# Second chunk's transposes on the DMA queue, logits in groups of two products, and the last residual added at evacuation

## The chip, the cores and the metric

The kernel runs on one core of one Trainium2 chip. The metric is the device time of one execution in microseconds (us), median of several runs. Engines are called by the names of the profile: PE is TensorE (PEld its weight loads), DVE is VectorE, ACT is ScalarE, POOL is GpSimd, SP is SyncE, which here only issues DMAs. A "q" after the name (SPq, ACTq) means the engine's instruction queue when it issues a DMA.

## The reference

The input is 2048 tokens of width 640 in bfloat16. Each row is normalised to xn, and the result is the sum of three parts: x itself, an attention branch and a feed-forward branch, both on xn.

```python
qkv = xn @ wqkv                       # 32 heads of 20
idx = pos[:, None] - 2*arange(8)      # each token sees itself and 7 others, 2 apart
logits = einsum(q, k[idx]) * 20**-0.5 # -1e9 where idx < 0
o = einsum(softmax(logits), v[idx])
h = gelu(xn @ w1 + b1)                # 640 -> 1536
out = x + o @ wo + (h @ w2 + b2)
```

## The kernel before

**Chunks and blocks.** The 2048 tokens are four chunks of 512 (n = 0 to 3), each of four blocks of 128 (bl = 0 to 3). Activations are held transposed, features on partitions and tokens along the free axis, so that a chunk's projection is a matmul with 512 columns.

**Stages of one chunk.** Statistics of x (st, DVE) and their square root (ACT) give xn (chunk 0 on DVE, the others on ACT, L398 to L409). xn has two buffers. It is then transposed into xnT: for chunks 0 and 1 by five PE matmuls a block against an identity (tp, L416) and an ACT copy from PSUM (tc, L420), for chunks 2 and 3 by a DMA transpose that SP issues (td, L428). Fifteen projections give q, k and v (for chunk 0 per block: gj, L472; for others pj, L455), copied out by ACT (pc, L490).

**Attention.** For each of the eight offsets w, DVE multiplies q with a shifted k (qk, L505). Two offsets share one product tile; there are four such tiles (pool "prod"), which also serve the products with v. A logits task (lg, L517) sums the 20 features of each head of one product tile by 20 matmuls with a 128x32 matrix of ones: 5 feature tiles times 4 token blocks, each block written to its own 32 partitions of L. In chunk 0 a mask is added to L for the first tokens by one more matmul for each two product tiles (L527). Then follow maximum (m, L540), difference (z, L547), exponential (ACT), sum, reciprocal and the weights attn on DVE. DMAs on SP and ACT repeat attn over the features of a head (ax, L584), DVE multiplies with shifted v (av, L600), adds (L609), and writes oT (L615), which has one buffer.

**Feed-forward and output.** Twelve tasks f1 (L622) with a GELU each (ge, ACT, L633) give hT; 18 buffers hold hT. A block's output needs five tasks o (pc 0 to 4; L655 for columns 0 to 511, "lo", L657 for the other 128, "hi"): pc 0 to 3 multiply hT with w2, pc 4 multiplies oT with wo. ACT copies lo and hi to osb (oc, L662), and a DMA issued by POOL adds osb to the output in memory (od, L668). What it adds to was stored before: x + b2, computed on DVE from x_sb and b2bc (xb, L432) and stored by SP (L439). The very last block, LASTB, does not go this way: its x + b2 is not stored, but added in PSUM, by two matmuls of x_sb against the identity, in pc 3:

```python
if pc == 3 and n * BPC + bl == LASTB:
    srcs.append((ident[:], x_sb[:, n * BPC + bl, :]))
```

Its lo half is computed first, copied by ACT and stored by SP (oclo, L676), while its hi half is still computed (ohi); then DVE copies hi (ochi, L685) and ACT's queue stores it.

**Order.** All instructions of PE, DVE and ACT are issued in one fixed order per engine, found when the kernel is built. `make_plan` adds tasks with an engine, an assumed duration, a rank, the tasks they need, the buffers they hold, and for some a time `after` which they may start. `Plan.run` then plays time forward: whenever an engine is free it starts the ready task with the smallest rank for which buffers are left. The table RANK adds offsets to the ranks of named groups ("f12" is all f1 of chunk 2). On the chip only the order remains: each instruction starts when what it needs is there, and everything behind it on its engine waits with it. A fourth kind of task, "dq", stands for the DMA queue in the plan.

**Loads.** Before anything else SP issues all loads in this order: x of chunk 0 and wq, wk, wv, then b1, x of the other chunks, w1, w2, wo and b2bc (L316 to L329). SP is not among the engines with a fixed order; 40 matmuls on the identity (L694) open PE's work.

Of the kernel before, what the change touches and what calls it, by code (L numbers as in the profile page):

```python
# [11 lines left out]
ALU = mybir.AluOpType  # L12
# [6 lines left out]
class Plan:  # L19
# [37 lines left out]
    def run(self):  # L57
        end, left, held = {}, list(self.tasks), {p: {} for p in self.pools}
        remaining = {b: set(u) for b, u in self.bufs.items()}
        free = {PE: 0.0, VE: 0.0, SE: 0.0, DQ: 0.0}  # L60
        now, started, table = 0.0, [], "sqrt"
        running, slacks = [], {t["slack"] for t in self.tasks}
        while left:
            done = [t for t in running if t["end"] <= now + 1e-9]
            for t in done:
                running.remove(t)
                for b in t["bufs"]:
                    remaining[b].discard(t["name"])
                    if not remaining[b]:
                        held[b[0]].pop(b, None)  # L70
            moved = True
            while moved:
                moved = False
                for eng in (PE, VE, SE, DQ):
                    if free[eng] > now + 1e-9:
                        continue
                    best = None
                    for t in left:
                        if t["eng"] != eng or t["after"] > now:
                            continue  # L80
                        if best is not None and (t["rank"], t["i"]) >= (best["rank"], best["i"]):
                            continue
                        if any(
                            n not in end
                            or end[n] + t["slack"] + (self.LAG[self.by[n]["eng"]] if self.by[n]["eng"] != eng else 0.0) > now + 1e-9
                            for n in t["needs"]
                        ):
                            continue
                        new = {}
                        for b in t["bufs"]:  # L90
                            if b not in held[b[0]]:
                                new[b[0]] = new.get(b[0], 0) + 1
                        if any(len(held[p]) + k > self.pools[p] for p, k in new.items()):
                            continue
                        best = t
                    if best is not None:
                        left.remove(best)
                        best["start"], best["end"] = now, now + best["us"]
                        if best["table"] not in (None, table):
                            table = best["table"]  # L100
                            best["end"] += self.TABLE
                        end[best["name"]] = best["end"]
                        free[eng] = best["end"]
                        for b in best["bufs"]:
                            held[b[0]][b] = True
                        running.append(best)
                        started.append(best)
                        moved = True
            nxt = [f for f in free.values() if f > now + 1e-9]
            for late in slacks:  # L110
                ready = [e + late + self.LAG[self.by[n]["eng"]] for n, e in end.items()]
                nxt += [r for r in ready if r > now + 1e-9]
            nxt += [t["after"] for t in left if t["after"] > now + 1e-9]
            if left and not nxt:
                raise RuntimeError("no piece can start: " + ", ".join(t["name"] for t in left[:8]))
            if left:
                now = min(nxt)
        return started
# [3 lines left out]
P = 128  # L122
# [16 lines left out]


RANK = {
    "ad00": 178, "av2": 376.9, "f11": 47.4, "f12": 101.9, "f13": 56.6, "gj1": 41.2, "gj3": 41.9, "o01": -41.2,
    "o02": 33.3, "o13": 84.5, "o23": 46.4, "ot0": 75.1, "pc12": 58.9, "pj30": 33.5, "pj32": 57, "qk2": -89.4,
    "st2": 250.4, "tc1": -2.9, "xb0": 48.2,
}


def make_plan(fns, offsets=RANK):
# [16 lines left out]
    for n in range(NCH):  # L165
# [15 lines left out]
        for bl in range(BPC):  # L181
            xn, tp = ("xn", n, bl), ("acc", "tp", n, bl)
            pl.add(f"xn{n}{bl}", SE if n else VE, 0.81 if n else 0.42, early + -4.0 if n else -99, [f"rc{n}" if n else f"rc{n}{bl}"], f("xn", n, bl), [xn])
            if n > 1:
                pl.add(f"tc{n}{bl}", DQ, 4.0, early - 3.0, [f"xn{n}{bl}"], f("td", n, bl), [xn, xnT])
                continue
            pl.add(f"tp{n}{bl}", PE, 0.3, early + -3.0 if n else -99, [f"xn{n}{bl}"], f("tp", n, bl), [xn, tp])
            pl.add(f"tc{n}{bl}", SE, 0.65, early + -3.0 if n else -99, [f"tp{n}{bl}"], f("tc", n, bl), [tp, xnT])
        pl.add(f"xb{n}", VE, 1.43, base + 36, [f"xn{n}{bl}" for bl in range(BPC)], f("xb", n), after=32.0)

        if n == 0:
            for bl in range(BPC):
# [19 lines left out]
        for wp in range(W // 2):  # L212
            pr = ("prod", "qk", n, wp)
            for i in range(2):
                need = done(n, 0) + done(n, 1) + [f"pad{n}1"]
                pl.add(f"qk{n}{wp}{i}", VE, 1.42, base + 3.0 * wp + i, need, f("qk", n, wp, i), [q, k, pr])
            pl.add(f"lg{n}{wp}", PE, 0.65, n - 1000, [f"qk{n}{wp}{i}" for i in range(2)] + ([f"lg{n}{wp-1}"] if wp else []), f("lg", n, wp), [pr, L], slack=0.8)

        e, at, ax = ("e", n), ("attn", n), ("ax", n)
        m, rs, ss, z = ("m", n), ("rs", n), ("ss", n), ("prod", "z", n)  # L220
# [24 lines left out]
        for bl in range(BPC):  # L245
# [2 lines left out]
            final = n * BPC + bl == LASTB  # L248
            last = None
            for pc in range(5):  # L250
                need = [last] if last else [f"ge{n}{ft}" for ft in range(FT)] + [f"xb{n}"]
                if pc == 4:
                    need.append(f"ot{n}")
                us = (0.65, 0.65, 0.65, 0.87, 1.08)[pc] if final else (0.82, 0.82, 0.82, 0.82, 1.37)[pc]
                last = pl.add(f"o{n}{bl}{pc}", PE, us, base + PERIOD + 8.0 + 8.0 * bl, need, f("o", n, bl, pc, ("lo",) if final else ("lo", "hi")), O + (hTs if pc == 0 else hTs[3 * pc : 3 * pc + 3] if pc < 4 else [oT]), 31.0)
            if final:
                pl.add("oclo", SE, 0.55, base, [last], f("oclo"), O + [ob])
                last = pl.add("ohi", PE, 1.05, base + PERIOD + 90, [last], f("ohi"), O)
                pl.add("ochi", VE, 0.25, base, [last], f("ochi"), O + [ob])
                continue  # L260
# [6 lines left out]
def kernel(  # L267
# [56 lines left out]
        cs = slice(n * BPC, (n + 1) * BPC)  # L324
        nc.sync.dma_start(x_sb[:, cs, :], x_nb[:, cs, :])
    nc.sync.dma_start(w1_sb[:], B_w1.rearrange("(t p) n -> p t n", p=P))
    nc.sync.dma_start(w2_sb[:], B_w2.rearrange("(t p) n -> p t n", p=P))
    nc.sync.dma_start(wo2[:], A_wo.rearrange("(p t) n -> p t n", t=KT))
    nc.sync.dma_start(b2bc[:], b2_bcast)  # L329


    ident = consts.tile([P, P], BF16, name="ident")
# [178 lines left out]

    def do_lg(n, wp):
        L = get(("L", n), lambda: psL.tile([P, W, P], F32, tag="L", name="L"))
        prod = tiles["qk", n, wp]
        for t in range(KT):
            for j in range(BPC):
                nc.tensor.matmul(  # L517
# [4 lines left out]
                    stop=(t == KT - 1 and wp % 2 == 1),  # L522
                    skip_group_check=True,
                )
        if n == 0 and wp % 2 == 1:
            g = slice(2 * wp - 2, 2 * wp + 2)
            nc.tensor.matmul(  # L527
                L[0:H, g, 0:MW],
                lhsT=ones_r[:],
                rhs=maskrow[:, g, :],  # L530
                start=False,
                stop=False,
                skip_group_check=True,
            )


    def do_max(n):
# [100 lines left out]
    def do_o(n, bl, pc, parts):  # L638
# [6 lines left out]
        lo, hi = tiles["lo", n, bl], tiles["hi", n, bl]  # L645
        if pc < 4:
            srcs = [(tiles["hT", n, ft][:, cs], w2_sb[:, ft, :]) for ft in range(3 * pc, 3 * pc + 3)]
            if pc == 3 and n * BPC + bl == LASTB:
                srcs.append((ident[:], x_sb[:, n * BPC + bl, :]))
        else:  # L650
            srcs = [(tiles["oT", n][:, t, cs], wo2[:, t, :]) for t in range(KT)]
        for k, (lhs, rhs) in enumerate(srcs):
# [20 lines left out]
    def do_oclo():  # L673
        osb = outp.tile([P, D], BF16, tag="osb", name="osb")
        tiles["osb", last] = osb
        nc.scalar.copy(osb[:, 0:CH], tiles["lo", *last][:])  # L676
        nc.sync.dma_start(out_sd[LASTB * P :, 0:CH], osb[:, 0:CH])

    def do_ohi():
# [2 lines left out]

    def do_ochi():
        osb = tiles["osb", last]
        nc.vector.tensor_copy(osb[:, CH:D], tiles["hi", *last][:, 0 : D - CH])  # L685
        nc.scalar.dma_start(out_sd[LASTB * P :, CH:D], osb[:, CH:D])

    fns = {k[3:]: v for k, v in locals().items() if k.startswith("do_")}
    engines = {mybir.EngineType.PE, mybir.EngineType.DVE, mybir.EngineType.Activation}
    with tc.manual_schedule(engines=engines):  # L690

        idle = psA.tile([P, CH], F32, tag="acc", name="idle")
# [34 lines left out]
```

## Time and profile before

| | |
|---|---|
| time, median of 3 runs | 218.56 us (218.47 to 218.74) |
| span of the profiled run | 216.7 us, TensorE clock 1.0 |
| PE busy | 209.4 us (97%) |
| DVE busy | 180.2 us (83%) |
| ACT busy | 110.6 us (51%) |
| POOL busy | 14.5 us (7%) |
| 512-column matmuls (L455, L622, L655) | record of 379 ns each |
| 128-column matmuls (L416, L472, L657) | record of 219 ns each |
| logits matmuls (L517) | 320, record of about 273 ns each |
| products of DVE (L505, L600) | 64, 1.48 us each |
| w1 issued, landed | 8.7, 23.1 us |
| DMA transposes (L428) | 8, landing 2.6 us after issue, the slowest 5.6 |

The span is the time between the first and the last instruction of one execution. The records of successive matmuls overlap[...]; the distance from start to start says what each one costs. Rows of a timeline give start, duration, engine, line, operation, the tile written and the tiles read, the shapes and how many such instructions are merged; in square brackets stands how long the engine sat idle before and who released it.

### The profile page before, as it was taken

What the parts mean: (1) busy time and instruction counts of PE and PEld (TensorE: products, weight loads), DVE (VectorE), ACT (ScalarE), POOL (GpSimd) and SP (SyncE); (2) the same over time, 40 slices, a digit from 0 to 9 for tenths busy, and PEclk for the clock granted to TensorE, in tenths of its full rate; (3) what the DMA queues carried; (4) which work ended last, traced back from release to release, by engine and by line L of the source; (5) the groups of instructions that cost most, each with busy time, mean ns of one, the idle gap of its engine ahead of it and who ended that gap; (6) DMA issues with size and microseconds to landing.
All of it is one profiled execution on the core that took longest, in us unless ns stands there. A gap on an engine that the chain in (4) does not pass through costs nothing.

```text
span 216.7 us, 3977 instructions
## 1 busy us (share of the span) xinstructions
PE 209.4 (97%) x1689; PEld 121.1 (56%) x1714; DVE 180.2 (83%) x169; ACT 110.6 (51%) x195; POOL 14.5 (7%) x33
## 2 busy tenths in 40 slices
PE   7899999999999999999999999999999999999994
PEld 7799855554554555555555455554544555555552
DVE  3759999988999999999899999989999999922000
ACT  3665999796757554734184625026665311341211
POOL 2000000000000000101010101011010011101121
PEclk9999999999999999999999999999999999999999
DMA  6999931907314401336020280222025222200253
GB/s 221 366 365 393 375 136 48 259 0 185 72 30 118 97 0 44 77 57 170 3 30 0 30 193 3 30 33 29 2 33 107 87 30 33 28 2 3 30 61 62
DMA packets 18761, 20.83 MB, mean 96 GB/s; under 512 B 6328, under 2 KB 15928, under 8 KB 18744
## 3 DMA queue, kind: packets, MB, share of 16 engines
q1 hardware_dynamic: 15144, 15.83, 24.7%
q0 software_dynamic: 2160, 2.46, 9.4%
q10 hardware_dynamic: 1440, 2.29, 3.1%
q8 instruction: 13, 0.21, 0.4%
q14 instruction: 4, 0.03, 0.0%
HBM read 10.00 MB, written 5.08 MB: 70 GB/s over the span
## 4 chain that ended last, share of the span: by engine, by line
PE 93%; DVE 1%; ACT 1%; DMA 1%; ACTq 1%; issue 1%; DVEq 0%
PE lo L655 27%; PE pps L455 23%; PE hps L622 22%; PE gps L472 8%; PE hi L657 8%; PE L L517 5%; DMA x_sb<-in_A_x_dram 1%; PE tp L416 1%; ACTq L584 1%; ACT L633 1%; DVE stats L375 0%; DVE stats L376 0%; ACT xnT L420 0%; ACT hT L633 0%; DVE xn L402 0%
## 5 line engine op out<-in xcount | busy, mean ns | idle before, releaser
L622 PE MATMUL hps<-xnT,w_sb 128*128 128x512 bf16 x230 | 53.2, 379 | 0.4
L655 PE MATMUL lo<-w_sb,hT 128*128 128x512 bf16 x187 | 52.9, 379 | 0.0
L505 DVE TENSOR_TENSOR prod<-qT,kT 128x2560 bf16<-128x2560 bf16 x32 | 45.4, 1483 | 0.7 <-ACT kT L490 0.7
L600 DVE TENSOR_TENSOR pv<-vT,ax 128x2560 bf16<-128x2560 bf16 x32 | 45.7, 1484 | 0.0
L657 PE MATMUL hi<-w_sb,hT 128*128 128x128 bf16 x192 | 40.3, 219 | 0.5 <-issue 0.3
L622 PEld LDWEIGHTS <-w_sb 128*128 128x128 bf16 x240 | 22.8, 98 | 26.3 <-issue 0.2
L633 ACT ACTIVATE hT<-hps,b1T 128x512 bf16<-128x512 f32 x48 | 31.4, 686 | 11.8 <-PE hps L622 9.8
L662 ACT CAST osb<-lo 128x512 bf16<-128x512 f32 x15 | 8.8, 586 | 53.8 <-PE hi L657 35.4
L609 DVE TENSOR_TENSOR pv<-pv 128x5120 bf16<-128x5120 bf16 x12 | 33.9, 2823 | 0.3
L655 PEld LDWEIGHTS <-hT 128*128 128x128 bf16 x192 | 18.7, 98 | 23.0 <-issue 1.5
L668 POOL DMA_DIRECT2D out_dram<-osb x15 | 13.1, 873 | 196.8 <-ACT osb L663 196.8
L655 PE MATMUL lo<-wo,oT 128*128 128x512 bf16 x75 | 22.1, 379 | 0.0
L657 PEld LDWEIGHTS <-hT 128*128 128x128 bf16 x192 | 18.4, 98 | 1.8
L455 PE MATMUL pps<-xnT,wv_sb 128*128 128x512 bf16 x74 | 17.3, 379 | 0.3 <-ACT hT L633 0.2
L657 PE MATMUL hi<-wo,oT 128*128 128x128 bf16 x80 | 16.9, 219 | 0.3
L455 PE MATMUL pps<-xnT,wk_sb 128*128 128x512 bf16 x74 | 16.8, 379 | 0.1
L455 PE MATMUL pps<-xnT,wq_sb 128*128 128x512 bf16 x72 | 16.7, 379 | 0.2
L490 ACT CAST vT<-pps 128x512 bf16<-128x512 f32 x15 | 8.7, 586 | 11.4 <-PE pps L455 9.4
L655 PEld LDWEIGHTS <-oT 128*128 128x128 bf16 x80 | 7.8, 98 | 9.6 <-issue 0.4
L455 PEld LDWEIGHTS <-wk_sb 128*128 128x128 bf16 x75 | 8.7, 118 | 7.3 <-issue 0.2
L455 PEld LDWEIGHTS <-wq_sb 128*128 128x128 bf16 x75 | 8.6, 118 | 7.1
L455 PEld LDWEIGHTS <-wv_sb 128*128 128x128 bf16 x75 | 8.5, 118 | 7.3 <-issue 0.5
(67 smaller groups left out, 208.9 us busy)
## 6 DMA issues: line engine op xcount, KB each, us to landing
w_sb<-in_B_w_dram SPq DMA_DIRECT2D x2, 1920.0 KB, 16.2
out_dram<-osb POOLq DMA_DIRECT2D x15, 160.0 KB, 3.4
ax<-attn SPq DMA_DIRECT2D x8, 256.0 KB, 4.9
ax<-attn ACTq DMA_DIRECT2D x8, 256.0 KB, 5.6
x_sb<-in_A_x_dram SPq DMA_DIRECT2D x3, 640.0 KB, 11.2
out_dram<-x_sb SPq DMA_DIRECT2D x3, 640.0 KB, 3.9
wq_sb<-in_A_wqkv_dram SPq DMA_DIRECT2D x1, 800.0 KB, 5.2
wk_sb<-in_A_wqkv_dram SPq DMA_DIRECT2D x1, 800.0 KB, 7.3
```

What stands on the lines that cost most here:

```text
L455: nc.tensor.matmul(ps[:], lhsT=wqkv_p[which][:, ti, to, :], rhs=xnT[:, ti, :], start=(ti == 0), stop=(ti == KT - 1),)
L472: nc.tensor.matmul(ps[:, i, :], lhsT=wqkv_p[which][:, ti, to, :], rhs=tiles["xnT", 0][:, ti, cs], start=(ti == 0), stop=(ti == KT - 1),)
L505: nc.vector.tensor_tensor(out=prod[:, i, :, :], in0=qkv_tile(n, 0)[:], in1=qkv_tile(n, 1)[:, :, off : off + CH], op=ALU.mult,)
L517: nc.tensor.matmul(L[j * H : (j + 1) * H, 2 * wp : 2 * wp + 2, :], lhsT=head_of[:], rhs=prod[:, :, t, j * P : (j + 1) * P], start=(t == 0 ...
L600: nc.vector.tensor_tensor(out=pv[:, i, :, :].rearrange("p t (j c) -> p t j c", j=BPC), in0=qkv_tile(n, 2)[:, :, off : off + CH].rearrange( ...
L609: nc.vector.tensor_tensor(out=ta[:], in0=ta[:], in1=tb[:], op=ALU.add)
L622: nc.tensor.matmul(ps[:], lhsT=w1_sb[:, ti, ft * P : (ft + 1) * P], rhs=tiles["xnT", n][:, ti, :], start=(ti == 0), stop=(ti == KT - 1),)
L633: nc.scalar.activation(hT[:], tiles["hps", n, ft][:], ACT.Gelu_apprx_tanh, bias=b1T[:, ft : ft + 1], scale=1.0)
L655: nc.tensor.matmul(lo[:], lhsT=lhs, rhs=rhs[:, 0:CH], start=first, stop=last)
L657: nc.tensor.matmul(hi[:, 0 : D - CH], lhsT=lhs, rhs=rhs[:, CH:D], start=first, stop=last)
L662: nc.scalar.copy(osb[:, 0:CH], tiles["lo", n, bl][:])
L668: nc.gpsimd.dma_start(rows, tiles["osb", n, bl][:], accum_op=ALU.add)
```

## The change

The change has five parts. The PE transposes and copies of chunk 1 are replaced by DMA transposes, as chunks 2 and 3 have them. The loads of w2, wo and b2bc become a task "ld", which SP issues only after chunk 1's transposes, so that these don't queue behind 2.9 MB of weights; SP's order is then fixed with that of the other engines, and the bias addition xb and the first o task wait for "ld" instead of for a fixed time. The logits task takes two product tiles at once: 40 matmuls in a row instead of twice 20, so that PE changes less often between the 128x128 and the 128x32 form. The last block's residual is added by DVE while it copies lo and hi out of PSUM, instead of by two matmuls; lo's copy moves from ACT to DVE for it. The offsets in RANK are others, so the order of tasks on every engine can differ.

```diff
-    "ad00": 178, "av2": 376.9, "f11": 47.4, "f12": 101.9, "f13": 56.6, "gj1": 41.2, "gj3": 41.9, "o01": -41.2,
-    "o02": 33.3, "o13": 84.5, "o23": 46.4, "ot0": 75.1, "pc12": 58.9, "pj30": 33.5, "pj32": 57, "qk2": -89.4,
-    "st2": 250.4, "tc1": -2.9, "xb0": 48.2,
+    "ad02": 35.3, "av1": -101.7, "av2": 76.7, "f10": 53.1, "f11": 23.2, "f12": 66, "f13": 190, "gj1": -337.3,
+    "gj3": -98.6, "o01": -72.1, "o03": 12.1, "o22": 213.2, "pj11": -45.8, "pj30": 109.2, "pj32": 49.6, "qk1": 10.4,
+    "qk2": 112.3, "rc1": -399, "st2": 79.8, "xb1": -67.6, "xb3": 55.5, "xn1": 47.4,
...
-            if n > 1:
-                pl.add(f"tc{n}{bl}", DQ, 4.0, early - 3.0, [f"xn{n}{bl}"], f("td", n, bl), [xn, xnT])
+            if n > 0:
+                pl.add(f"tc{n}{bl}", DQ, 4.0 if n > 1 else 2.7, early - 3.0, [f"xn{n}{bl}"], f("td", n, bl), [xn, xnT], 21.5)
...
-        pl.add(f"xb{n}", VE, 1.43, base + 36, [f"xn{n}{bl}" for bl in range(BPC)], f("xb", n), after=32.0)
+        if n == 1:
+            pl.add("ld", DQ, 9.2, -1000, [f"tc1{bl}" for bl in range(BPC)], f("ld"))
+        pl.add(f"xb{n}", VE, 1.43, base + 36, [f"xn{n}{bl}" for bl in range(BPC)] + ["ld"], f("xb", n))
...
-            pl.add(f"lg{n}{wp}", PE, 0.65, n - 1000, [f"qk{n}{wp}{i}" for i in range(2)] + ([f"lg{n}{wp-1}"] if wp else []), f("lg", n, wp), [pr, L], slack=0.8)
+            if wp % 2:
+                both = [("prod", "qk", n, wp - 1), pr]
+                need = [f"qk{n}{x}{i}" for x in (wp - 1, wp) for i in range(2)] + ([f"lg{n}{wp-2}"] if wp > 2 else [])
+                pl.add(f"lg{n}{wp}", PE, 1.2, n - 1000, need, f("lg", n, wp), both + [L], slack=0.8)
...
-                pl.add("oclo", SE, 0.55, base, [last], f("oclo"), O + [ob])
+                pl.add("oclo", VE, 0.65, base, [last], f("oclo"), O + [ob])
...
+    def do_ld():
+        nc.sync.dma_start(w2_sb[:], B_w2.rearrange("(t p) n -> p t n", p=P))
+        nc.sync.dma_start(wo2[:], A_wo.rearrange("(p t) n -> p t n", t=KT))
+        nc.sync.dma_start(b2bc[:], b2_bcast)
...
     def do_lg(n, wp):
-        prod = tiles["qk", n, wp]
+        for x in range(2):
+            prod = tiles["qk", n, wp - 1 + x]
+            logits(L, prod, wp - 1 + x)
...
-            if pc == 3 and n * BPC + bl == LASTB:
-                srcs.append((ident[:], x_sb[:, n * BPC + bl, :]))
...
-        nc.scalar.copy(osb[:, 0:CH], tiles["lo", *last][:])
+        nc.vector.tensor_tensor(out=osb[:, 0:CH], in0=tiles["lo", *last][:], in1=x_sb[:, LASTB, 0:CH], op=ALU.add)
...
-        nc.vector.tensor_copy(osb[:, CH:D], tiles["hi", *last][:, 0 : D - CH])
+        nc.vector.tensor_tensor(
+            out=osb[:, CH:D], in0=tiles["hi", *last][:, 0 : D - CH], in1=x_sb[:, LASTB, CH:D], op=ALU.add
+        )
...
-    engines = {mybir.EngineType.PE, mybir.EngineType.DVE, mybir.EngineType.Activation}
+    engines = {getattr(mybir.EngineType, e) for e in ("PE", "DVE", "Activation", "SP")}
```

More of the change, by code (lines that the diff above doesn't have):

```diff
@@ L78, in run @@
                     for t in left:
-                        if t["eng"] != eng or t["after"] > now:
+                        if t["eng"] != eng or t["after"] > now + 1e-9:
                             continue
@@ L250, in make_plan @@
             for pc in range(5):
-                need = [last] if last else [f"ge{n}{ft}" for ft in range(FT)] + [f"xb{n}"]
+                need = [last] if last else [f"ge{n}{ft}" for ft in range(FT)] + [f"xb{n}", "ld"]
                 if pc == 4:
                     need.append(f"ot{n}")
-                us = (0.65, 0.65, 0.65, 0.87, 1.08)[pc] if final else (0.82, 0.82, 0.82, 0.82, 1.37)[pc]
-                last = pl.add(f"o{n}{bl}{pc}", PE, us, base + PERIOD + 8.0 + 8.0 * bl, need, f("o", n, bl, pc, ("lo",) if final else ("lo", "hi")), O + (hTs if pc == 0 else hTs[3 * pc : 3 * pc + 3] if pc < 4 else [oT]), 31.0)
+                us = (0.65, 0.65, 0.65, 0.65, 1.08)[pc] if final else (0.82, 0.82, 0.82, 0.82, 1.37)[pc]
+                last = pl.add(f"o{n}{bl}{pc}", PE, us, base + PERIOD + 8.0 + 8.0 * bl, need, f("o", n, bl, pc, ("lo",) if final else ("lo", "hi")), O + (hTs if pc == 0 else hTs[3 * pc : 3 * pc + 3] if pc < 4 else [oT]))
             if final:
-                pl.add("oclo", SE, 0.55, base, [last], f("oclo"), O + [ob])
+                pl.add("oclo", VE, 0.65, base, [last], f("oclo"), O + [ob])
                 last = pl.add("ohi", PE, 1.05, base + PERIOD + 90, [last], f("ohi"), O)
@@ L326 @@
     nc.sync.dma_start(w1_sb[:], B_w1.rearrange("(t p) n -> p t n", p=P))
-    nc.sync.dma_start(w2_sb[:], B_w2.rearrange("(t p) n -> p t n", p=P))
-    nc.sync.dma_start(wo2[:], A_wo.rearrange("(p t) n -> p t n", t=KT))
-    nc.sync.dma_start(b2bc[:], b2_bcast)
+    def do_ld():
+        nc.sync.dma_start(w2_sb[:], B_w2.rearrange("(t p) n -> p t n", p=P))
+        nc.sync.dma_start(wo2[:], A_wo.rearrange("(p t) n -> p t n", t=KT))
+        nc.sync.dma_start(b2bc[:], b2_bcast)
     ident = consts.tile([P, P], BF16, name="ident")
@@ L513, in do_lg, with logits @@
         L = get(("L", n), lambda: psL.tile([P, W, P], F32, tag="L", name="L"))
-        prod = tiles["qk", n, wp]
+        for x in range(2):
+            prod = tiles["qk", n, wp - 1 + x]
+            logits(L, prod, wp - 1 + x)
+        if n == 0:
+            g = slice(2 * wp - 2, 2 * wp + 2)
+            nc.tensor.matmul(
+                L[0:H, g, 0:MW],
+                lhsT=ones_r[:],
+                rhs=maskrow[:, g, :],
+                start=False,
+                stop=False,
+                skip_group_check=True,
+            )
+    def logits(L, prod, wp):
         for t in range(KT):
@@ L524, in do_lg @@
                 )
[L525 to L534, printed above, removed]
     def do_max(n):
@@ L684, in do_ochi @@
         osb = tiles["osb", last]
-        nc.vector.tensor_copy(osb[:, CH:D], tiles["hi", *last][:, 0 : D - CH])
+        nc.vector.tensor_tensor(
+            out=osb[:, CH:D], in0=tiles["hi", *last][:, 0 : D - CH], in1=x_sb[:, LASTB, CH:D], op=ALU.add
+        )
         nc.scalar.dma_start(out_sd[LASTB * P :, CH:D], osb[:, CH:D])
     fns = {k[3:]: v for k, v in locals().items() if k.startswith("do_")}
-    engines = {mybir.EngineType.PE, mybir.EngineType.DVE, mybir.EngineType.Activation}
+    engines = {getattr(mybir.EngineType, e) for e in ("PE", "DVE", "Activation", "SP")}
     with tc.manual_schedule(engines=engines):
```

## The prediction

> **What bounds the kernel now.** I read the page first (busy times, the 40 slices, the chain), then the timeline of TensorE around each kind of work that the change touches, then the waits of VectorE, then the DMA landings.
>
> ```profile
> PE 209.4 (97%) x1689; PEld 121.1 (56%) x1714; DVE 180.2 (83%) x169; ACT 110.6 (51%) x195; POOL 14.5 (7%) x33
> ...
> PE   7899999999999999999999999999999999999994
> ...
> DVE  3759999988999999999899999989999999922000
> ...
> PE 93%; DVE 1%; ACT 1%; DMA 1%; ACTq 1%; issue 1%; DVEq 0%
> ```
>
> TensorE is full from the third slice to the last but one, and the chain that ends last is 93% TensorE. VectorE is nearly as full, but only up to about 190 us; then it waits for TensorE. A busy share alone doesn't prove a bound here, because records of consecutive matmuls overlap. So I took start-to-start distances. In steady stretches a 512-column matmul follows the last after 0.216 us and a 128-column one after 0.056 us. From 12 us to the last matmul (start 213.34) I find only one pause over 0.1 us that isn't a missing record or a change to logits: 0.36 us at 53 us, where a PSUM buffer waits for a GELU behind a table load. TensorE has no slack: what is taken from it leaves the time, unless it starts to wait.
>
> The stretch in which all of chunk 1's transposes lie, by the timeline of TensorE:
>
> ```profile
> 27.63 0.81 PE L622 MATMUL hps<-xnT,w_sb 128*128 128x512 bf16 x3
> 28.37 0.73 PE L517 MATMUL L<-prod,head_of 128*32 128x256 bf16 x20
> 29.03 0.73 PE L416 MATMUL tp<-ident,xn 128*128 128x128 bf16 x10
> ...
> 31.85 0.73 PE L517 MATMUL L<-prod,head_of 128*32 128x256 bf16 x20
> 32.51 0.20 PE L527 MATMUL L<-maskrow,ones_r 1*32 1x64 bf16 x1
> 32.64 1.25 PE L622 MATMUL hps<-xnT,w_sb 128*128 128x512 bf16 x5
> 33.73 0.44 PE L416 MATMUL tp<-ident,xn 128*128 128x128 bf16 x5
> 34.10 0.73 PE L517 MATMUL L<-prod,head_of 128*32 128x256 bf16 x20
> 34.77 0.45 PE L416 MATMUL tp<-ident,xn 128*128 128x128 bf16 x5
> ```
>
> Three things are to be seen. The transposes (L416) stand in the stream and cost their 0.056 us each. A logits group (L517) starts late: the last hps matmul starts at 27.63 + 0.81 - 0.38 = 28.06, its successor was due at 28.28, and L starts at 28.37, 0.09 late. And after the group's last matmul (start 28.37 + 0.73 - 0.27 = 28.83) the next one starts only at 29.03, 0.20 later. The tail of the kernel:
>
> ```profile
> 211.10 0.38 PE L655 MATMUL lo<-x_sb,ident 128*128 128x512 bf16 x1
> ...
> 211.31 1.24 PE L655 MATMUL lo<-wo,oT 128*128 128x512 bf16 x5
> ...
> 212.64 0.59 ACT L676 CAST osb<-lo 128x512 bf16<-128x512 f32 x1 [1.89 <-issue]
> 213.06 0.22 PE L657 MATMUL hi<-x_sb,ident 128*128 128x128 bf16 x1
> ...
> 213.65 0.29 DVE L685 CAST osb<-hi 128x128 bf16<-128x128 f32 x1 [14.05 <-PE hi L657]
> ```
>
> The two identity matmuls that add the last block's residual are on the path; the end hangs on hi, not on lo.
>
> **What the Trainium skill says.** "TensorEngine Tiling (Array Packing)", section Key Properties: changing the tiling mode drains the engine. The trace agrees: 0.09 + 0.20 us around each 128x32 group, where the same tile shape continues without such a gap. "TensorE: Matmul & The Clock Gate", section "Wait — 56ns, not 53.3ns?", gives 55.6 and 215.7 ns between starts at 128 and 512 columns; this trace has 56 and 216. "DMA: Bandwidth & Descriptors", section "Queues, rings and completion order": each DMA engine takes a ring's descriptors in order. The trace agrees: w1 (issued 8.7) landed 14.4 us later, w2 (issued 10.5) 18.0, wo (12.6) 17.9, b2bc (21.0) 9.9, that is at 23.1, 28.5, 30.5 and 30.9, in order of issue. That is why w2, wo and b2bc are put behind the transposes.
>
> **The change part by part.**
> (1) Chunk 1's transposes leave TensorE: 4 blocks x 5 x 0.056 = 1.1 us off the path. On ScalarE four copies of 0.69 us go (2.8 us at 29.5 to 36), which is off the path. In their place come four DMA transposes in SyncE's order. Their price is in the trace for chunks 2 and 3:
>
> ```profile
> L428 SPq DMA_TRANSPOSE xnT<-xn x8: 1200/1278/2051, 38.2 to 72.5; - x8
> ...
> DMA to landing us min/median/max: 2.6/2.6/5.6
> ```
>
> xn has two buffers, so they go in two pairs. In the kernel before the first two xn of chunk 1 end at 23.9 and 25.35. From 25.35: landing +2.6, the next two xn (ScalarE, 0.91 each) +1.9, landing +2.6, a third SyncE issue +1.3: about 33.8. With the worst landing (5.6, twice) 39.8. The readers are pj1 on TensorE, at 38.1 before. Until then it has twelve f1 of chunk 0 (12 x 5 x 0.216 = 13.0 us) and chunk 0's logits (2.8 us) from 25.0 on, that is work to 40.8. So I cost the new wait at 0, hidden by f1 of chunk 0; upper bound: a planner's order is fixed at build time, so TensorE can stand before pj1 although f1 is left, up to 39.8 - 33.8 = 6 us.
> (2) w2, wo, b2bc leave SyncE only after the transposes are issued, about 33 us. They are 2.9 MB; at the 365 to 393 GB/s of the loading slices that is 7.6 us plus some 2 us of latency: 43. Behind them on SyncE wait the stores of x + b2 and half of the ax copies, which were at 48.8. The first o matmuls with w2 start at 55.2, so this is hidden by projections and f1. The two bias additions that filled VectorE's wait for logits (34.77 to 37.7, just before m at 38.20) can't run so early; stats of another chunk (four times 1.0 us, at 40.6 to 43.6 before) can. VectorE loses 0 to 3 us; I take 1.
> (3) Logits in groups of two. One group costs 0.09 in, 0.46 between its first and last start (five rounds of four tiles, 0.11 a round), 0.20 out = 0.75 us. Two apart: 1.51. Two together: 0.09 + 0.46 + 0.10 + 0.46 + 0.20 = 1.31. So 0.195 a pair, eight pairs: 1.56 us. Bounds: 0.1 (the last round overlaps the exit) to 0.3 a pair, 0.8 to 2.4 us. The new wait: the first product now stays in its buffer until the second is made. m waits for a group of 1.2 instead of 0.66 us, so VectorE may idle 0.55 us longer in each of four chunks, 2.2 in all, unless other products fill it, as pv does before chunk 2's and 3's m.
> (4) The two identity matmuls: 0.216 + 0.056 = 0.27 off the path. lo's evacuation moves to VectorE, which is idle there. z of 128x1024 float32 from PSUM took 1.22 us, a first half by columns about 0.69. It starts at about the time of the ScalarE cast, 0.7 + 0.3 us after which hi is ready, so hi's addition isn't held up. A second operand on hi (0.29 us) is costed at 0, at most 0.1.
> (5) New rank offsets, no forced times for xb and o. They remove no work; they move it. I can't derive their order from the profile: 0 if TensorE stays fed, some us if not.
> Sum: 1.1 + 1.56 + 0.27 = 2.95 us. 218.56 - 2.95 = 215.6 with the 0.36 us pause kept. I add 0.3 us of new short waits: 215.9.
>
> **Rivals.** What speaks against the full sum is how close VectorE is. Its oT of chunk 2 is done at 169.48 + 1.49 = 170.97, and the first o matmul that reads it starts at 172.97: 2.0 us. For chunk 1 it is 131.17 against 131.95, for chunk 0 83.64 against 84.51. VectorE's longest waits:
>
> ```profile
> DVE oT L615 <- PE hi L657: 7.3, 1, 7.3
> DVE m L540 <- PE L L517: 1.2, 2, 0.6
> ```
>
> A. TensorE's saving stays: 215.9. For it: no waits of TensorE now, and 7.3 us of slack on VectorE at the end.
> B. Part is paid back, because TensorE, 2.7 us ahead by chunk 2 and with VectorE 1 to 3 us later, waits for oT, or for the transposes: at 170 us, 2.7 + 1 - 2.0 = 1.7 us. 215.6 + 1.7 = 217.3.
> C. The fixed order puts pj1 before the transposes land, or loses VectorE time at the load: 3 to 6 us of waits, 215.6 + 3.5 = 219.1, to 221.6. Slower. For it: the 5.6 us landing; against it: f1 as filler, and w1 landed by 23.1.
> D. The pauses at 53 us and the head's (0.3 + 0.4 us before 7.4) shrink as well and the grouping gives 0.3 a pair: 214.5.
>
> **How the numbers follow.** A 0.61, B 0.22, C 0.10, D 0.07. The likeliest is A, so 215.9. The range, 8 in 10, reaches over A and most of B on the long side and half of D on the other: 214.8 to 217.8. "Within 0.2%" is 218.1 to 219.0. A and D are faster, and nearly all of B (217.3 with 0.7 about it, 0.02 into "same"); C is parted between same (0.03) and slower (0.07). Faster 0.88, same 0.05, slower 0.07.
>
> **What would show it.** In the profile after: no L416 after 12 us, twelve DMA transposes, the third and fourth landed by about 34; L517 eight times in forties with 1.2 to 1.3 us to the next matmul; no x_sb into lo or hi; TensorE busy about 206.5 with pauses under 1 us in all after 12 us; TensorE's end near 210.6 and the same 3.1 us of tail. I am wrong if TensorE waits over 1.5 us for xnT, oT or a product, if the first start after a forty lies more than 1.4 us after its first, or if VectorE's addition of lo delays that of hi.

## The result and the profile after

The change makes the kernel faster, by a little over half of what was forecast: 217.04 us (216.83 to 217.82, 5 runs) against 218.71, ratio 0.9936 [0.9911, 0.9961] (the ratio takes in all runs; the two medians alone give 0.992). A second set of runs gave 217.29 us (5 runs), ratio 0.9926 [0.9911, 0.9941]. The forecast was 215.9.

The page of the kernel after; the order of the lines is that of the page before:

```profile
PE 208.0 (96%) x1669; PEld 121.6 (56%) x1692; DVE 180.8 (84%) x170; ACT 107.2 (50%) x190; POOL 14.5 (7%) x33
...
PE   7799999999999999999999999999999999999994
...
DVE  3649899769989999999999999998999999982001
...
PE 48%; DVE 28%; DMA 16%; SPq 3%; issue 2%; ACTq 1%; ACT 1%; DVEq 0%
```

The slices still say that TensorE is full. The last line doesn't: of the chain that ended last, TensorE now holds 48% where it held 93%, and VectorE and DMAs hold 44%. So there are places where TensorE was held up by something else. First the work that was to go from TensorE, by its timeline:

```profile
26.50 6.64 PE L634 MATMUL hps<-xnT,w_sb 128*128 128x512 bf16 x29
33.07 1.28 PE L539 MATMUL L<-prod,head_of 128*32 128x256 bf16 x40
34.27 0.20 PE L527 MATMUL L<-maskrow,ones_r 1*32 1x64 bf16 x1
34.41 2.33 PE L634 MATMUL hps<-xnT,w_sb 128*128 128x512 bf16 x9
36.58 2.32 PE L463 MATMUL pps<-xnT,wk_sb 128*128 128x512 bf16 x10
```

No transposes are left in it, and chunk 1's projections (L463) follow f1 without a pause. The logits come in forties. The last hps matmul before them starts at 26.50 + 6.64 - 0.38 = 32.76, its successor was due at 32.98, L starts at 33.07, and the next start after the forty is at 34.27: 0.09 + 1.20 = 1.29 us. In a chunk without the mask, a forty costs 1.30 us by the same reading, and a single twenty in the kernel before 0.755: 0.209 us saved a pair (forecast 0.195). In chunk 0 it is 0.755 + 0.883 for two twenties, the second with the mask, against 1.43. Taken one by one, the eight pairs give 1.69 us. The tail, all engines:

```profile
211.70 0.83 PE L667 MATMUL hi<-w_sb,hT 128*128 128x128 bf16 x12
211.96 0.69 DVE L686 TENSOR_TENSOR osb<-lo,x_sb 128x512 bf16<-128x512 f32 x1 [16.09 <-PE lo L665]
212.37 0.44 PE L667 MATMUL hi<-wo,oT 128*128 128x128 bf16 x5
212.68 0.35 SPq L687 DMA_DIRECT2D out_dram<-osb  x1
212.85 0.29 DVE L695 TENSOR_TENSOR osb<-hi,x_sb 128x128 bf16<-128x128 f32 x1 [0.20 <-PE hi L667]
```

The two identity matmuls are gone. The addition of lo took 0.69 us, as forecast, and was over 0.2 us before hi was ready. The chain of waits in order of time, where it leaves TensorE (columns: start, length, what):

```profile
26.93 4.06 PE hps L634 x18
...
35.32 10.10 DMA b2bc<-in_B_b_dram
45.44 1.49 DVE x_sb L440
46.94 1.86 DVE ssum L574
48.82 0.96 DVE rs L581
49.80 1.23 DVE attn L586
...
115.46 7.02 DVE pv L612 x5
122.50 0.59 ACTq L596
123.13 1.68 ACTq L596
124.86 0.59 ACT vT L498
125.49 1.24 PE pps L463 x5
```

Read it from below. At 125.5 us TensorE's projections of v had waited for a copy by ScalarE, whose queue was held by two DMA issues (ACTq L596, the ax copies). These could not go out before VectorE's five products (115.46 to 122.48) had read the only ax buffer. The pieces left out between are VectorE's work and the ax transfers that it waits for, back to the bias addition xb at 45.44 (L440), and that waited for b2bc, the last of the three postponed loads.

The first profile after and the one before also differ at the head: f1 starts at 26.50 against 25.04. That is chance and not the change: in the repeated profile of the kernel after it starts at 25.14, and one kernel below that keeps the order of the kernel before has it at 26.24. Below I therefore count from the first f1 to the start of the last matmul, "the stretch": 188.30 us before, 186.09 and 186.66 in the two profiles after.

### The profile page after: what moved, and what is told of

Read it like the earlier page. It is cut to its first block, busy times and chain, and to the rows that moved or that the text cites. A ratio compares the mean times of both kernels' runs of the same rounds, so it can differ in the third digit from the quotient of the medians.

```text
span 215.8 us, 3941 instructions
## 1 busy us (share of the span) xinstructions
PE 208.0 (96%) x1669; PEld 121.6 (56%) x1692; DVE 180.8 (84%) x170; ACT 107.2 (50%) x190; POOL 14.5 (7%) x33
## 4 chain that ended last, share of the span: by engine, by line
PE 48%; DVE 28%; DMA 16%; SPq 3%; issue 2%; ACTq 1%; ACT 1%; DVEq 0%
PE lo L665 18%; PE hps L634 14%; DVE pv L612 10%; PE gps L480 6%; DMA ax<-attn 6%; PE hi L667 6%; DMA wv_sb<-in_A_wqkv_dram 5%; DMA b2bc<-in_B_b_dram 5%; DVE pv L621 4%; DVE prod L513 3%; PE pps L463 3%; DVE ssum L574 3%; DVE x_sb L440 2%; DVE attn L586 2%; DVE rs L581 1%
## 5 line engine op out<-in xcount | busy, mean ns | idle before, releaser
L634 PE MATMUL hps<-xnT,w_sb 128*128 128x512 bf16 x236 | 54.2, 379 | 0.2
L665 PE MATMUL lo<-w_sb,hT 128*128 128x512 bf16 x183 | 51.9, 379 | 0.0
L621 DVE TENSOR_TENSOR pv<-pv 128x5120 bf16<-128x5120 bf16 x12 | 33.8, 2824 | 0.3
L665 PE MATMUL lo<-wo,oT 128*128 128x512 bf16 x77 | 22.6, 379 | 0.0
L463 PE MATMUL pps<-xnT,wv_sb 128*128 128x512 bf16 x72 | 17.2, 379 | 0.4 <-ACT vT L498 0.3
L463 PE MATMUL pps<-xnT,wk_sb 128*128 128x512 bf16 x71 | 16.9, 380 | 0.3
L463 PE MATMUL pps<-xnT,wq_sb 128*128 128x512 bf16 x75 | 16.8, 379 | 0.2 <-ACT qT L498 0.2
L383 DVE BATCH_NORM_STATS2 stats<-x_sb 128x6 f32<-128x320 bf16 x16 | 7.4, 460 | 8.4 <-DMA x_sb<-in_A_x_dram 8.4
L686 DVE TENSOR_TENSOR osb<-lo,x_sb 128x512 bf16<-128x512 f32 x1 | 0.7, 692 | 16.1 <-PE lo L665 16.1
L498 ACT CAST vT<-pps 128x512 bf16<-128x512 f32 x15 | 8.2, 596 | 11.3 <-PE pps L463 11.3
L463 PEld LDWEIGHTS <-wq_sb 128*128 128x128 bf16 x75 | 8.8, 117 | 7.8 <-issue 0.5
```

Of the source, the lines that this page charges most:

```text
L463: nc.tensor.matmul(ps[:], lhsT=wqkv_p[which][:, ti, to, :], rhs=xnT[:, ti, :], start=(ti == 0), stop=(ti == KT - 1),)
L498: nc.scalar.copy(dest[:, to, off : off + CH], tiles["pps", n, which, to][:])
L621: nc.vector.tensor_tensor(out=ta[:], in0=ta[:], in1=tb[:], op=ALU.add)
L634: nc.tensor.matmul(ps[:], lhsT=w1_sb[:, ti, ft * P : (ft + 1) * P], rhs=tiles["xnT", n][:, ti, :], start=(ti == 0), stop=(ti == KT - 1),)
L665: nc.tensor.matmul(lo[:], lhsT=lhs, rhs=rhs[:, 0:CH], start=first, stop=last)
```

## The experiments

Ratios are to the kernel before on the same chip. "TensorE's waits" are its pauses after 26 us, taken from start-to-start distances over what the same shapes cost without a pause; they are 0.14 us in the kernel before, at 53 us. The prediction read 0.36 there; one of the twenty matmuls just before has no record, and its 0.216 us are no wait.

**Both kernels again, and the head.** The first two runs change nothing.

> The kernel before, unchanged, for the scatter of its first 25 us. In the profile before, the first f1 matmul started at 25.04 us; in the profile after at 26.50, with k's weights landing 1.3 us later, and transposes at half speed at 6.4 to 7.2. Theory 'chance': such a late start is a matter of the single execution and hits this kernel too; over its executions the times spread by up to 1 us, and some have a mean clock of 0.999. Theory 'order': it comes from the changed order of the first projections; then this kernel starts f1 at 25.0 again and its times lie within 0.4 us.

218.80 us (13 runs), ratio 0.9998 [0.9988, 1.0008]; stretch 188.31, waits 0.15.

> The changed kernel, unchanged. Between the first f1 and the last matmul the profile after has 186.1 us, the one before 188.3; both theories expect 186.1 +- 0.2 again, with about 1.07 us of TensorE waits in it (0.37 and 0.22 near 76 us, 0.43 near 125 us). Theory 'chance': first f1 between 25.0 and 26.5, differing from the first profile; median about 217.0 with two groups of times near 216.9 and 217.8. Theory 'order': first f1 at 26.0 or later again.

217.29 us; stretch 186.66, over the 186.1 +- 0.2 expected, waits 1.65. The three largest are 0.54 at 74.7, 0.63 at 123.9 and 0.22 at 76.3 us. In the first profile after they were at 75.9, 124.9 and 77.3, 1.07 in all: the same places, with sizes that vary from one execution to the next.

```diff
...
-    "gj1": -337.3, "gj3": -98.6,
+    "gj1": 41.2, "gj3": 41.9,
...
```

> The changed kernel with the rank offsets of chunk 0's projections (gj1, gj3) as in the kernel before; the rest of the order is the same. Theory 'order': first f1 back at 25.0 to 25.2 us, median lower than the changed kernel's by 0.8 to 1.4 us. Theory 'chance': no difference beyond 0.3 us.

217.25 us (6 runs), ratio 0.9931 [0.9915, 0.9948], f1 at 25.30, waits 1.72. The ranks of the first projections are not what made the head of the first profile late.

**One part alone: the logits.** The kernel before, with the two twenties of a pair issued together:

```diff
+        if wp % 2 == 0:
+            return
+        for x in range(2):
+            logits(L, tiles["qk", n, wp - 1 + x], wp - 1 + x)
...
```

> The kernel before with one part of the change: the logits matmuls of two products are issued together, at the place of the second; every other instruction stays in its order. The prediction's step (3): 0.755 us twice becomes 1.30, so eight pairs save 1.6 to 1.7 us: 217.0. The rival: products are held longer and m waits longer, so that VectorE, fixed in its order, runs up to 2.2 us later and TensorE gives the saving back at oT: 218.0 to 218.7.

217.27 us (5 runs), ratio 0.9937 [0.9922, 0.9952]: this part alone gives what the whole change gives. Its stretch is 186.98. Worked out: 188.30 - 1.69 (the eight pairs) + 0.47 (waits 0.61 instead of 0.14) = 187.08. Most of the waits is one of 0.46 us at 96.9, where a copy out of PSUM stands behind the issue of ax copies in ScalarE's queue (at 93.9, 2.4 us). So the grouping, too, brings a small wait with it.

**The load of b2bc.** The kernel after, with b2bc first of the three postponed loads:

```diff
     def do_ld():
+        nc.sync.dma_start(b2bc[:], b2_bcast)
         nc.sync.dma_start(w2_sb[:], ...)
         nc.sync.dma_start(wo2[:], ...)
-        nc.sync.dma_start(b2bc[:], b2_bcast)
```

> The changed kernel, with b2bc as the first of the three postponed loads instead of the last; nothing else moves. In the profile of the changed kernel VectorE waits 2.4 us at its first bias addition for b2bc, and from there on runs 1.4 to 2 us behind. Theory 'VectorE': that lag holds ScalarE up (its copy of v's first columns at 74 us waits for VectorE's products, its ax DMAs at 121 us wait for attn), and TensorE then waits for ScalarE's copies out of PSUM, 1.65 us in all after 26 us. Then here the wait for b2bc is gone or under 0.5 us, VectorE is 1.3 us earlier from 46 us on, TensorE's waits after 26 us fall to 0.3 to 0.6 us, and the time is 216.0 to 216.4. Rival 'ScalarE': the waits come from ScalarE's own durations and table loads; then TensorE's waits stay at 1.4 to 1.7 and the time at 217.0 to 217.4.

215.87 us (215.40 to 216.19, 4 runs), ratio 0.9874 [0.9860, 0.9887]: 1.4 us less than the 217.29 of the kernel after (1.1 by the two ratios), from one line moved, and a little less than theory 'VectorE' expected. The transfer itself, by the landing times of the DMAs (last column: us from issue to landing), in the kernel after and then here:

```profile
b2bc<-in_B_b_dram SPq DMA_DIRECT2D x1, 160.0 KB, 10.1
```

```profile
b2bc<-in_B_b_dram SPq DMA_DIRECT2D x1, 160.0 KB, 4.6
```

VectorE in the repeated kernel after, then in this one:

```profile
40.16 1.22 DVE L559 TENSOR_TENSOR z<-L,m 128x1024 f32<-128x1024 f32 x1
...
44.40 1.49 DVE L440 TENSOR_TENSOR x_sb<-x_sb,b2bc 128x2560 bf16<-128x2560 bf16 x1 [2.45 <-DMA b2bc<-in_B_b_dram]
45.81 1.93 DVE L574 TENSOR_REDUCE ssum<-e 128x128 f32<-128x1024 bf16 x1
```

```profile
40.05 1.22 DVE L559 TENSOR_TENSOR z<-L,m 128x1024 f32<-128x1024 f32 x1
...
41.76 1.48 DVE L440 TENSOR_TENSOR x_sb<-x_sb,b2bc 128x2560 bf16<-128x2560 bf16 x1
44.07 1.94 DVE L574 TENSOR_REDUCE ssum<-e 128x128 f32<-128x1024 bf16 x1 [0.82 <-ACT e L569]
```

z starts within 0.11 us in both. In the kernel after xb, put between z and the sum to fill the time of the exponential, stands for 2.45 us before a load that isn't there, and everything behind it starts 45.81 - 44.07 = 1.74 us later. With b2bc in time, xb is done before the exponential is. TensorE's waits fall from 1.65 to 0.22, and the stretch is 185.23. The chain of this kernel has TensorE back at most of it, and b2bc nowhere:

```profile
PE 78%; DVE 14%; DMA 4%; ACTq 1%; issue 1%; ACT 1%; SPq 0%; DVEq 0%
```

**The same lateness by other means.** If VectorE's lateness is what counts and not the load as such, it must cost the same when something else makes it. The kernel with b2bc first, and in chunk 0 the sum over the exponentials computed twice (the second gives the same values):

```diff
+        for _ in range(2 if n == 0 else 1):
             nc.vector.tensor_reduce(out=ssum[:], in_=...)
```

> b2bc first, as in after_b2 (215.87 us, TensorE's waits 0.22 us), and chunk 0's sum over e computed twice: 1.93 us more for VectorE at 44 us, the output unchanged. It is the converse of after_b2. Theory 'VectorE': VectorE is 1.9 us later from there on, as it was behind by 1.75 us at this place in the changed kernel; TensorE's waits after 26 us return to 1.4 to 2.0 us, near 75 and 124 us; the time is 217.0 to 217.6. Rival: TensorE's supply of other work hides it (VectorE waits 7.3 us for oT near the end in the kernel before): 215.9 to 216.2.

217.40 us (22 runs), ratio 0.9944 [0.9931, 0.9956], stretch 187.41, waits 2.40: the time is as theory 'VectorE' expected, the waits are above its 1.4 to 2.0. The extra sum takes 1.93 us of VectorE; 1.5 us of it comes out as time. TensorE's waits by line (us in total, times, longest):

```profile
PE pps L463 <- ACT vT L498: 1.0, 2, 0.6
PE pps L463 <- ACT qT L498: 0.6, 1, 0.6
```

They are at 75.0 and 124.4 (and a short one at 51.5), the places of the kernel after, though b2bc has landed in time. So VectorE's lateness at 46 us is enough to cause them. The loss also follows the lateness: counted from the first f1, the reciprocal behind chunk 0's sum starts 1.3 us later than with b2bc first in the first profile after, 1.6 in the repeated one and 2.0 here, and the stretch is 0.86, 1.43 and 2.18 us longer.

**How it reaches TensorE.** The waits name ScalarE, not VectorE. Around 74 us in the repeated kernel after, all engines:

```profile
72.31 2.75 PE L463 MATMUL pps<-xnT,wq_sb 128*128 128x512 bf16 x12
72.94 0.59 ACT L498 CAST qT<-pps 128x512 bf16<-128x512 f32 x1 [0.49 <-PE pps L463]
...
74.65 0.25 ACT L505 COPY vT<-vT 128x70 bf16<-128x70 bf16 x1 [1.13 <-DVE pv L612]
74.81 0.58 ACT L498 CAST qT<-pps 128x512 bf16<-128x512 f32 x1
...
75.44 1.24 PE L463 MATMUL pps<-xnT,wq_sb 128*128 128x512 bf16 x5 [0.38 <-ACT qT L498]
```

ScalarE stands for 1.13 us before a small copy of v's border (L505), which goes into the buffer of chunk 0's v (v has two buffers) that VectorE's products still read. Behind it in the queue is the copy of q out of PSUM, and TensorE wants that buffer. Two runs try to take out one link each, in the kernel after. The border copies on GpSimd:

```diff
-            nc.scalar.copy(dest[:, :, 0:PAD], ...)
+            nc.gpsimd.tensor_copy(dest[:, :, 0:PAD], ...)
```

> The changed kernel, with the copies of the previous chunk's last columns of k and v made by GpSimd instead of ScalarE. Theory 'VectorE': TensorE's waits near 75 us (0.6 to 0.75) go, but TensorE then comes 0.7 us earlier to the place near 124 us, where ScalarE waits for attn of a VectorE that isn't earlier, and waits that much longer there: waits after 26 us still 1.4 to 1.7 in all, time 217.0 to 217.4. Rival 'ScalarE': the waits are independent of each other; 0.7 us are gained: 216.5.

217.62 us (6 runs), ratio 0.9959 [0.9945, 0.9973], waits 1.83. The wait at 75 us is gone, and there is no gain, because it comes out elsewhere: not near 124 us, as expected, but at oT. TensorE's timeline:

```profile
81.54 1.24 PE L463 MATMUL pps<-xnT,wv_sb 128*128 128x512 bf16 x5
83.49 0.39 PE L665 MATMUL lo<-wo,oT 128*128 128x512 bf16 x1 [0.70 <-DVE oT L627]
```

Now the o tasks stand before oT itself: VectorE is no earlier, and TensorE has only walked on to the next place where it needs VectorE. The ax copies all on SyncE, none in ScalarE's queue:

```diff
-        expand(nc.scalar, n, (2, 3))
+        expand(nc.sync, n, (2, 3))
```

> The changed kernel, with all four ax copies of a chunk issued by SyncE instead of two of them by ScalarE. Theory 'VectorE': ScalarE no longer stands before its ax DMAs at 117 to 124 us until attn is ready, so TensorE's wait near 124 us (0.43 to 0.63) goes; the waits near 75 us (0.6 to 0.75) stay: 216.6 to 216.9. Rival: the copies land up to 1.2 us later, VectorE waits for ax, and TensorE loses it elsewhere: 217.2 to 218.

217.41 us (22 runs), ratio 0.9953 [0.9937, 0.9969]: no gain either; here the rival came true. ScalarE's queue is free and the wait near 124 us is gone. (What the ax copies had stood for there is not attn, as the expectations say: in the repeated kernel after attn is done at 114.6 us, and the copies go out at 121.7, when VectorE's products have read the only ax buffer.) But the copies now go out one behind another, and VectorE waits for them. By VectorE's waits:

```profile
DVE pv L612 <- DMA ax<-attn: 2.6, 3, 1.9
DVE x_sb L440 <- DMA b2bc<-in_B_b_dram: 2.6, 1, 2.6
```

The repeated kernel after has 0.8 us in place of the first line. TensorE's waits are 2.47, of which 2.19 at 74.6, in a profiled execution of 218.23 us, 0.8 above the median. The same move with b2bc first:

> b2bc first and ax on SyncE together. Theory 'VectorE': both causes removed, TensorE's waits after 26 us at most 0.3 us, the time 215.5 to 216.0. Rival 'ScalarE': as with ax on SyncE alone, 216.6 to 216.9.

215.83 us (5 runs), ratio 0.9868 [0.9854, 0.9882], the same as b2bc first alone. The profile is of the longest execution (216.82 us), with waits of 0.66, over the expected 0.3. VectorE waits 2.6 us for the ax copies here too, 0.8 with b2bc first alone, and this lateness is largely made up: counted from the first f1, VectorE is 1.4 us behind that kernel after a wait for ax at 104.6 us, but only 0.6 from the last chunk's maximum on, before which that kernel waits 0.56 us for logits and this one doesn't. The stretch is 0.44 us longer.

**Transposes and the place of the loads.** The kernel after, with w2, wo and b2bc back among the first loads:

```diff
     nc.sync.dma_start(w1_sb[:], ...)
+    nc.sync.dma_start(w2_sb[:], ...)
+    nc.sync.dma_start(wo2[:], ...)
+    nc.sync.dma_start(b2bc[:], b2_bcast)
...
```

> The changed kernel with w2, wo and b2bc loaded ahead of everything again, as in the kernel before; the order on the other engines is the same. What the postponement is worth: if the transposes queue behind 2.9 MB, the first pair, issued at 20.8 and 22, lands at about 31 instead of 24 to 25; the third xn (24.6 in the plan) waits for its buffer with ScalarE's copies and GELUs behind it, so TensorE runs out of PSUM buffers by 28 us and waits 3 to 5 us: 219 to 222. Rival: the transposes' packets get between the loads', they land within 4 us, b2bc is there early and VectorE isn't held: 215.8 to 216.2.

223.41 us (6 runs), ratio 1.0230 [1.0203, 1.0256], more than expected; stretch 193.88, waits 8.84. The first transposes queue behind the weights, ScalarE's third xn waits 7.22 us for the xn buffer they hold, and TensorE 5.77 us for copies behind that xn. Three stretches (columns: us, busy us of PE, PEld, DVE, ACT, POOL, granted TensorE clock, DMA share, GB/s):

```profile
25.00:33.00 8.00, 2.36 (x14) 1.07 (x13) 8.00 (x7) 1.26 (x2) 0.00 (x0) 0.93 0.94 236
33.00:38.50 5.50, 5.32 (x13) 1.87 (x13) 4.74 (x11) 4.42 (x9) 0.00 (x0) 0.50 0.15 30
38.50:45.00 6.50, 6.45 (x64) 3.38 (x64) 0.00 (x0) 3.39 (x5) 0.00 (x0) 0.98 0.13 26
```

The pause costs twice: after it the clock is granted at half, and 13 matmuls start 0.427 us apart instead of 0.216. Postponing the loads is thus worth some 6 us here (223.41 - 217.29). In the order of the kernel before, it would not have been needed. There, only the transposes of chunk 1 go to DMAs, and all loads stay in front:

```diff
     def do_tp(n, bl):
+        if n:
+            return
...
     def do_tc(n, bl):
+        if n:
+            return do_td(n, bl)
```

> The kernel before with chunk 1's transposes made by DMA and nothing else: all loads stay in front, every other instruction in its order. The prediction's step (1) takes 1.1 us from TensorE: 217.5. Rival: the transposes land behind the loads at 31 us, xn's third block waits for its buffer on ScalarE with GELUs behind it, and pj1 (38.1 before) waits: 218.7 or more.

218.19 us (7 runs), ratio 0.9968 [0.9951, 0.9985], between the two expectations. The transposes are issued from 25.1 us on instead of 20.8, the second lands at 32.2 behind the loads, and TensorE doesn't wait for them. The stretch is 187.69: 1.11 us saved, 0.50 us of new waits (0.65, one of 0.45 at 98.8 us).

**The tail alone.** The kernel before, with the last residual added at evacuation:

```diff
-            if pc == 3 and n * BPC + bl == LASTB:
-                srcs.append((ident[:], x_sb[:, n * BPC + bl, :]))
...
-        nc.scalar.copy(osb[:, 0:CH], tiles["lo", *last][:])
+        nc.vector.tensor_tensor(out=osb[:, 0:CH], in0=..., in1=x_sb[:, LASTB, 0:CH], op=ALU.add)
```

> The kernel before with the last block's residual added by VectorE at evacuation and nothing else. The prediction's step (4): 0.27 us less: 218.4. Rival: hi's addition or lo's is held up behind the other on VectorE and the store goes out as late as before: 218.7. In the trace the last matmul should start 0.27 us earlier and hi's addition end 0.3 us after hi.

218.86 us (22 runs), ratio 1.0008 [1.0001, 1.0015]: no gain. The stretch is 188.05, so TensorE did save 0.25 us, but from the start of the last matmul to the end it is 3.72 us instead of 3.31. The landing of the last two stores (lo, hi):

```profile
out_dram<-osb SPq DMA_DIRECT2D x1, 128.0 KB, 2.3
out_dram<-osb ACTq DMA_DIRECT2D x1, 32.0 KB, 2.0
```

Before, they took 1.7 and 1.5 us. lo's store is now issued 0.08 us after the last matmul's start instead of 0.09 before it: the addition takes 0.69 us and ScalarE's copy took 0.59, and hi's group is shorter by its identity matmul of 0.056. Why the stores land later stays open. That the two slow each other by this timing doesn't explain it: in the whole change they are issued at the same points (0.08 and 0.58 us after the last matmul's start), hi's lands in 1.7 us and the tail is 3.2 us in both profiles.

## Why the prediction was right in direction and wrong in size

The direction was right and the time lies in the range; the size was not. By the prediction's own steps:

- **(1), transposes.** 20 x 0.056 = 1.11 us, as forecast. The fourth transpose was issued at 31.18 us in the repeated profile; its landing isn't in the trace, but with the third's 2.58 us it comes to about 33.8 (forecast 33.8), and chunk 1's first projection started at 35.2 without a wait. The cost of 0 for the new wait was right, and so was its reason. A loss of rival C's size, from late transposes, is what the run with all loads in front shows, there by way of ScalarE's xn, and not the change.
- **(2), postponed loads: the step that failed.** The landing was nearly right (forecast 43; 44.4 and 45.4 measured). The error is who waits for it, and what that costs. I called the loads "hidden by projections and f1", looking at what stands behind them on SyncE (48.8 us) and at the first reader of w2 on TensorE (55.2). I knew that the bias additions on VectorE can't run early, but did not ask where the new order has the first: at 42 us, in front of chunk 0's sum. It waited 2.1 and 2.4 us for b2bc. About 0.8 of that would have gone on waiting for the exponential, so VectorE came 1.3 and 1.6 us late, within "0 to 3 us; I take 1". What failed is the step from there to TensorE: I let VectorE's loss cost next to nothing there, and it cost 0.86 and 1.43 us, the difference in the stretch to the kernel with b2bc first.
- **(3), logits.** 1.69 us against 1.56 forecast. m waits 1.0 to 1.1 us once and 0.6 once for logits, where it waited 0.6 three times before: the added 0.55 a chunk is nearly reached in chunk 0, and in sum m waits no longer.
- **(4), residual.** 0.27 us off TensorE and the tail as it was, in the whole change. Alone, it gains nothing.
- **(5) and the sum.** What leaves TensorE is 1.11 + 1.69 + 0.27 = 3.07 us, against 2.95 forecast. "0.3 us of new short waits" is the mis-sized term, by the failed step of (2): measured 1.65 - 0.14 = 1.51 (repeated profile; 0.93 in the first). 3.07 - 1.51 = 1.56, and the stretch is 188.30 - 186.66 = 1.64 shorter. With b2bc first the new waits are 0.08, the sum gives 2.99, and the stretch is 3.07 shorter.

So rival B had the size, 217.3, and half of the mechanism. It had TensorE ahead of a late VectorE, but worked its 1.7 us out for a wait at oT near 170 us; that the number fits so well is luck. The lateness came from one load at 44 us, and the wait reached TensorE earlier and mostly through ScalarE's queue; at oT it appears only where that path was taken away. Rival A's second reason, VectorE's 7.3 us of slack before its last oT, did not hold either: that wait is 0.9 us in the new order. The forecast of 215.9 is met by the kernel with b2bc first, 215.87, 1.3% below the kernel before; only the run that moves the ax copies as well, 215.83, is as fast.

What stays open: why the residual alone loses at the tail what it gains before, and why VectorE's lateness, and with it the waits, differs between executions of one kernel.

## What to carry to other kernels

When loads are postponed, list for each one its first reader in the new order, on every engine, and issue first what is read first, above all where it is small. In a fixed order a stall of an engine that is 84% busy need not be absorbed: here the one at 44 us came out at the next places where the bound engine needed that engine, under the name of whatever stood between, and taking one such link away only moved the wait. The stall of 1.2 us at 104.6 us, with b2bc first and ax on SyncE, was mostly made up. So look, too, where the late engine would have waited anyway. Follow the chain of waits back to the first piece that isn't work.

## What the runs showed that I had not expected

- The place in the queue decided this small load's landing: 160 KB landed 10.1 us after issue behind w2 and wo, and 4.6 us when issued ahead of them. What I had taken from the Trainium skill, "DMA: Bandwidth & Descriptors", section "Queues, rings and completion order", for the sake of the transposes, that each DMA engine takes a ring's descriptors in order, covers this load as well, and these two times agree with it.
- With all loads in front, a pause of 5.8 us on TensorE was followed by 13 matmuls at 0.427 us instead of 0.216, some 2.7 us more.
- The last two stores of 128 and 32 KB landed in 1.7 and 1.5 us before, and in 2.3 and 2.0 with the residual alone added at evacuation.
